# Soft-capped attention, feed-forward and routed experts on one Trainium2 core: expert tiles grouped into pairs, singles and small remainders, with a general path in a branch and constants made after the start

## The chip, the cores and the metric

The kernel runs on one core of one Trainium2 chip. The metric is the device time of one execution in microseconds. Lower is better. The time before is the median of three executions.

## The reference

Three stages follow each other. All data is float32.

```python
scores = cap * np.tanh(scale * (q @ k.T) / cap)          # 4 batches, 12 heads, 448 rows, 64 columns
attn = softmax(scores) @ v                               # -> x of 1792 tokens x 768
h = x @ w_in; x = (h * sigmoid(1.702 * h)) @ w_out       # 768 -> 2048 -> 768
logits = x @ w_gate; e_idx = argmax(logits, axis=1)      # 8 experts, each token goes to one
for e in range(8):
    mask = e_idx == e
    h = np.maximum(x[mask] @ w1[e], 0.0)                 # 768 -> 1024
    out[mask] = gate_w[mask, None] * eom[mask, e, None] * (h @ w2[e])   # 1024 -> 768
```

For the inputs that the reference makes, the eight experts get 616, 5, 21, 4, 710, 134, 3 and 299 of the 1792 tokens. Of the first 1344 tokens (three of the four batches) expert 0 gets 517. These counts are the reference's own `argmax`, counted.

## The kernel before

A planner (class `Plan`) puts every operation of the kernel into a static order for each engine. Each operation is added with a cost, a due time `v` shifted by a table `LEAD`, the operations it depends on and the ring buffers it uses. `run` fills the engines by due time. The order is fixed when the kernel is built, so on the chip each engine works through its list and waits for semaphores. Rings (`Ring(n)`) are buffers that are handed out in turn: user number c may start when user number c - n has finished.

The prologue (lines 384 to 445) runs before the planner's list. It makes constants: `zer`, `carry`, the identity, several scalars from the cap, `epst`, `fold`, `ones`, `tri` and eight ranges by `iota_f` (an iota on GpSimd, then a copy to float on VectorE, through one shared buffer). The first halves of q and k (`ld_qk`, line 565) come by one DMA of the SP queue and one of the ACT queue. The one on the ACT queue stands behind the activations of the prologue on that engine.

Attention and the feed-forward network are interleaved batch by batch. Float32 products are made as sums of three one-pass products: each operand is split into a rounded high part (`rnd_any`, line 477, ScalarE or VectorE) and a remainder (`rest_any`, line 485, VectorE), and high x high, low x high and high x low are added up in PSUM.

The routing of a batch (`route`) ends with running expert counts in `carry` and with scatters of token numbers into tables (line 1100). The experts' stage works in tiles of 128 tokens of one expert, called slots. `NSLOT` = 21 is the most that can be needed. Three full tiles (`NEARLY`) are picked after the third batch, and the others are enumerated after the fourth by a chain of small VectorE operations (`enumerate_tiles`, `expert_ids`, `token_ids`), sorted by expert. Slot number 21 is computed at the end under a branch (`tc.If`, line 1564, `last_slot`), which these inputs don't take. A second branch (line 1570) holds a whole second program for very large caps, not taken either.

One slot is:

- `slot_in`: an indirect gather of 128 token rows (line 1372), six transposes on TensorE (line 1392), a split of the result into two tiles `xT`.
- `l1`: for each of six chunks of the contraction, three products times two halves of 512 columns (line 1422, 36 matmuls), both halves side by side in two PSUM banks `psF`. Then ReLU (line 1435), eight transposes (line 1440), a split into two tiles `gT`.
- `l2`: for each of eight chunks three products times two halves of 384 columns (line 1472, 48 matmuls), in one PSUM tile `psO` of two banks. Then `out_y` (line 1479, ScalarE) and an indirect scatter (line 1482).

The expert's weights are loaded by conditional DMAs on the SP queue (`w_load`, line 1323): 3 of 1024 KB for `w1` and 4 of 768 KB for `w2`, into seven raw buffers that exist once each. The condition is a register that says whether the expert differs from that of the tile before. Each of the 14 chunks is split for every slot (`w_split`: 6 of 128x1024 and 8 of 128x768), into a ring of `WFB` + `MWB` = 4 + 5 buffers. The slots are staggered: `l1` of slot s is followed by `l2` of slot s - 1.

Of the kernel before, what the change touches and what calls it, by code (L numbers as in the profile page):

```python
# [9 lines left out]
F32 = mybir.dt.float32  # L10
F32R = mybir.dt.float32r
# [30 lines left out]
LEAD = {'tanh': 2.01, 'v_hi': 11.65, 'pv2': -12.5, 'tr': 5.5, 'x2_cp': -19.75, 'relu': -13.28, 'th': 16.62, 'g_hi': 18.86, 'x2_hi': 4.05, 'x2_lo': -8.67, 'transp': 14.31, 'w_s': -4.08, 'cap_max': -1.12, 'v_lo': 3.85, 'mms': 4.36, 'x2_tr': 4.06, 'pv_x': -6.73, 'scores': 6.33, 'q_hi': -30.03, 'lo': -8.55, 'ld_qk': 13.3, 'o_acc': -2.83, 'g_lo': -11.44, 'k_hi': 0.43, 'exp': 8.98, 'p_hi': 3.53, 'eps': -29.31, 'quantum': -3.73, 'w_e': 4.47, 'st_': 1.6, 'hi': 7.17, 'gmul': -12.05, 'pv1': -4.48, 'pv_add': 11.51, 'pv_cp': 22.53, 'p_lo': 13.02, 'logit': -9.76, 'norm': -11.99, 'x_hi': 5.57, 'out_y': -2.47, 'o_x2': -0.32, 'w_1': -3.42, 'w_2': -7.23, 'x_lo': 2.89, 'recip': -28.64, 'ld': -11.81, 'ld_v': 1.27, 'k_lo': 2.18, 'q_lo': 2.48, 'u_cp': -6.08, 's_ld': 6.02, 's_rc': -0.15, 's_st': -6.55, 'r_ld': -20.47, 'f': 17.0, 'v_f': 0.29}  # L42
TICK = 10.24 / 3
WFR = 2
W1 = 123.44
W2 = 218.024
W3 = 306.814
AF1 = 0.664
AF2 = 0.711
AF3 = 0.715  # L50
AO1 = -2.008
AO2 = -30.195
AO3 = 38.993
WLEAD = 22.922
RESTD = 1.01
POOLD = 0
# [5 lines left out]
ATT0 = 2.581  # L62
HID = 0.031
F3 = 157.954
NORMD = 0.877
NEARLY = 3
# [4 lines left out]
GATH = 10.0  # L71
WPRE = 14.0
# [3 lines left out]
VPL = 1.869  # L76
STG = -3.554
GL = 37.536
XIN = 11.584
HL = 10.021  # L80
XAL = 79.95
SPLIT = True
CV0 = 129.09
CV1 = 54.183
MWB = 5
SLOT = 17.899
# [28 lines left out]
class Plan:  # L115
# [10 lines left out]
    def __init__(self):  # L126
        self.tasks = []
        self.free = {"POOL": 5.0, "DVE": 4.5, "SP": 0.7}
        self.port = 0.0
        self.active = {}  # L130
# [209 lines left out]

@with_exitstack
def tile_softcap_attention_ffn_moe(
# [44 lines left out]
    nc.scalar.activation(carry, zer[:, :NE], AF.Copy)  # L387
# [20 lines left out]
    nc.scalar.activation(epst, ncapa, AF.Exp)  # L408
    nc.vector.tensor_scalar(out=epst, in0=epst, scalar1=1e-9, scalar2=None, op0=ALU.mult)
# [4 lines left out]
    nc.vector.tensor_tensor(out=fold, in0=ident[:32, :16], in1=ident[:32, 16:32], op=ALU.add)  # L414


    ones = const.tile([CK, 128], BF16, name="ones")
    nc.vector.memset(ones, 1.0)
    tri32 = const.tile([CK, CK], F32, name="tri32")
    nc.vector.memset(tri32, 1.0)  # L420
# [7 lines left out]
    def iota_f(name, p, pattern, base=0, cm=0):  # L428
        n = 1
        for _, k in pattern:  # L430
            n *= k
# [1185 lines left out]
```

## Time and profile before

| | us |
|---|---|
| median of 3 executions | 1145.5 |
| lowest and highest | 1144.22, 1148.94 |
| the profiled execution | 1141.25 |
| its span, first to last instruction | 1139.5 |
| mean granted TensorE clock (1 is 2.4 GHz) | 0.992 |

The profiled execution lasted 1.75 us longer than its span, and 4.25 us less than the median. Busy time of TensorE is not a measure of how much it could do, because matmuls overlap and their ends are modelled; the distance between their starts tells more.

### The profile page before, as it was taken

The numbers are of one execution on the slowest core, as the hardware profiler recorded it, in microseconds if no ns is written. First come the engines' busy times: TensorE is split into PE (matmuls) and PEld (weight loads), VectorE is DVE, ScalarE is ACT, GpSimd is POOL, SyncE is SP. The second block draws the span as 40 slices with busy tenths as digits, with TensorE's granted clock in tenths as the row PEclk, the third lists the DMA queues.
The fourth block names the chain that finished last, engine by engine and source line by source line (L and its number), as shares of the span: only waits on it lengthen the run. The fifth ranks groups of instructions, "written<-read, shape, count | busy, mean of one in ns | idle before, by whom it ended". The sixth has DMA issues, their size and how long they took to land. (4 is left out here: it accounts for less than half of the span.)

```text
span 1139.5 us, 16349 instructions
## 1 busy us (share of the span) xinstructions
PE 1090.1 (96%) x5378; PEld 918.4 (81%) x5378; DVE 933.4 (82%) x1606; ACT 779.3 (68%) x1308; POOL 209.7 (18%) x158
## 2 busy tenths in 40 slices
PE   5999999999999989999999999998999999999996
PEld 2455777778888878888888888977999898989986
DVE  4797999998897576697895645679999999999993
ACT  6998798787885353477882233347888787878873
POOL 0111001000000200100000102004623424243340
PEclk9999999999999989999999999999999999999999
DMA  6887678788887742744422535430279721347601
GB/s 177 213 233 199 196 201 253 223 238 242 267 245 247 146 117 81 160 119 113 127 87 86 118 127 210 179 112 24 69 262 377 276 101 43 120 152 289 253 1 37
DMA packets 70848, 191.37 MB, mean 168 GB/s; under 512 B 11950, under 2 KB 22494, under 8 KB 70752
## 3 DMA queue, kind: packets, MB, share of 16 engines
q1 hardware_dynamic: 63872, 170.79, 49.5%
q0 software_dynamic: 6656, 19.19, 5.2%
q8 instruction: 45, 0.74, 0.3%
q14 instruction: 51, 0.42, 0.1%
q10 hardware_dynamic: 224, 0.23, 0.1%
HBM read 238.86 MB, written 29.08 MB: 235 GB/s over the span
## 5 line engine op out<-in xcount | busy, mean ns | idle before, releaser
L971 PE MATMUL fps<-xh,w 128*128 128x448 f32 x384 | 146.8, 382 | 8.7 <-ACT w L477 8.2
L1482 POOL DMA_INDIRECT out_dram<-y,si x20 | 109.8, 5491 | 179.8 <-ACT y L1479 171.2
L971 PE MATMUL fps<-gh,w 128*128 128x448 f32 x384 | 142.2, 370 | 0.3 <-DVE th L995 0.3
L973 PE MATMUL fps<-xh,w 128*128 128x448 f32 x384 | 141.4, 368 | 0.3 <-DVE w L485 0.3
L972 PE MATMUL fps<-xl,w 128*128 128x448 f32 x384 | 141.4, 368 | 0.0
L972 PE MATMUL fps<-gl,w 128*128 128x448 f32 x384 | 140.8, 367 | 0.0
L973 PE MATMUL fps<-gh,w 128*128 128x448 f32 x384 | 140.2, 365 | 0.0
L485 DVE TENSOR_TENSOR w<-w 128x768 fp32r<-128x768 f32 (+1 forms) x98 | 104.1, 1068 | 42.7 <-ACT w L477 42.3
L646 ACT ACTIVATE p<-p,capx 112x448 f32<-112x448 f32 x192 | 126.9, 674 | 2.1
L642 ACT ACTIVATE p<-sps 112x448 f32<-112x448 f32 x184 | 97.2, 543 | 32.0 <-PE sps L638 17.4
L1472 PE MATMUL ops<-mw,gT 128*128 128x384 f32 x540 | 101.9, 339 | 0.0
L637 PE MATMUL sps<-qks 128*112 128x448 f32 x184 | 80.5, 437 | 21.5 <-ACT vf L477 12.1
L1422 PE MATMUL hps<-mw,xT 128*128 128x512 f32 x390 | 97.0, 399 | 0.0
L1472 PEld LDWEIGHTS ops<-mw,gT 128*128 128x128 f32 x540 | 93.2, 188 | 0.1
L477 ACT ACTIVATE w<-w 128x768 fp32r<-128x768 f32 (+1 forms) x78 | 71.8, 924 | 31.1 <-DMA w<-wsp 31.1
L971 PEld LDWEIGHTS fps<-xh,w 128*128 128x128 f32 x384 | 72.7, 189 | 22.1 <-ACT w L477 9.0
L477 ACT ACTIVATE mw<-w2r 128x768 fp32r<-128x768 f32 x79 | 67.0, 848 | 33.9 <-PE hps L1422 29.1
L1422 PEld LDWEIGHTS hps<-mw,xT 128*128 128x128 f32 x390 | 73.3, 191 | 14.9
L485 DVE TENSOR_TENSOR mw<-w2r,mw 128x768 fp32r<-128x768 f32 x90 | 82.1, 956 | 2.9 <-ACT mw L477 2.4
L1422 PE MATMUL hps<-w,xT 128*128 128x512 f32 x330 | 82.3, 398 | 0.0
L485 DVE TENSOR_TENSOR mw<-w1r,mw 128x1024 fp32r<-128x1024 f32 x65 | 77.1, 1220 | 5.6 <-ACT mw L477 5.6
L971 PEld LDWEIGHTS fps<-gh,w 128*128 128x128 f32 x384 | 72.1, 188 | 11.0 <-DVE th L995 0.6
(222 smaller groups left out, 2386.4 us busy)
## 6 DMA issues: line engine op xcount, KB each, us to landing
w1r<-in_w_dram SPq DMA_DIRECT2D x60, 1024.0 KB
w2r<-in_w_dram SPq DMA_DIRECT2D x80, 768.0 KB
w<-wsp SPq DMA_DIRECT2D x56, 384.0 KB
w<-wsp SPq DMA_DIRECT2D x42, 512.0 KB
qkr<-in_qk_dram SPq DMA_DIRECT2D x95, 224.0 KB
wr<-in_w_in_dram SPq DMA_DIRECT2D x32, 384.0 KB
wr<-in_w_out_dram SPq DMA_DIRECT2D x24, 512.0 KB
x2s<-x2tok SPq DMA_DIRECT2D x4, 1358.0 KB
```

The source lines that it names most:

```text
L477: nc.scalar.activation(o, i, AF.Copy)
L485: e.tensor_tensor(out=o, in0=x, in1=f32(hi), op=ALU.subtract)
L637: mm(sps, lhsT=t[:, 1, sl], rhs=t[:, 0, :], start=True, stop=False)
L642: nc.scalar.activation(p, T["s", kc], AF.Tanh, scale=sct2[:CK] if qkf else 1.0)
L646: nc.scalar.activation(p, p, AF.Exp, scale=capx[:CK])
L971: mm(fps, lhsT=wh, rhs=xh, start=c == 0, stop=False)
L972: mm(fps, lhsT=wh, rhs=xl, start=False, stop=False)
L973: mm(fps, lhsT=wl, rhs=xh, start=False, stop=c == n - 1)
L1422: mm(T["h", s][n], lhsT=x_[:, kk, :], rhs=w[:, a, n * 512:(n + 1) * 512], start=st_, stop=sp_)
L1472: mm(T["o", s][:, n, :384], lhsT=x_[:, k, :], rhs=w[:, a, n * 384:(n + 1) * 384], start=st_, stop=sp_)
L1482: nc.gpsimd.indirect_dma_start(out=out[:, :], out_offset=bass.IndirectOffsetOnAxis(ap=M[f"si{g}"][:, i:i + 1], axis=0), in_=T["y", s].rear ...
```

## The change

The experts' stage works in units that share one split of an expert's weights. A unit is a pair (P, two tiles of 128 tokens), a single (S, one tile) or a remainder (T, up to 64 tokens). Two pairs are picked after the third batch; after the fourth follow four groups of three units in the fixed order P T S, P T S, P T T, P T T. That is 14 tiles of 128 tokens and 6 remainders. The weights are loaded (if the expert changed) and split once for a unit.

A remainder is computed in two passes in place of three. Its high part fills stationary columns 0 to 63 and its low part columns 64 to 127 of one tile. One matmul gives high x high and low x high in separate rows, a second one of 64 columns adds high x low. The two sets of rows are added up by a matmul with `fold2` (first layer) or by VectorE (`low_y`, `sum_y`, `scaled_y`, second layer).

In every tile the second half of the columns runs two chunks behind the first (`AHEAD`), and each half has its own PSUM bank: `psO` has two single-bank buffers. The ring of split weights has 4 + 6 buffers. The enumeration after the fourth batch (`late_units`, `cumulate`, `find`) works on three lists of eight experts.

Tokens that the fixed units don't cover are found by `uncovered`; then a branch at the end computes all tiles again with 21 `last_slot` bodies. The branch for slot 21 is gone. With the counts above the units cover every token: expert 0 takes two early pairs and a single, expert 4 three pairs, expert 5 a single and a remainder, expert 7 a pair and a remainder, and the others a remainder each.

`epst`, `fold`, `ones`, `tri` and the ranges are made as tasks of the planner with due time 40 (`late_constants`); new constants (`fold2`, unit numbers as 52 one-column GpSimd memsets in groups of six) are made there too. The planner's tuned numbers (`LEAD`, stage lengths and offsets) are other values throughout, so the order of work in attention and feed-forward changes too.

```diff
-LEAD = {'tanh': 2.01, 'v_hi': 11.65, 'pv2': -12.5, 'tr': 5.5, ...
+LEAD = {'tanh': 3.35, 'v_hi': 13.94, 'pv2': -3.72, 'tr': 5.5, ...
...
-NEARLY = 3
+NPE = 2
+UNITS1 = [x for i in range(4) for x in ((i, "P"), (6 + i, "T"), ((4, "S"), (5, "S"), (10, "T"), (11, "T"))[i])]
+SLOTS1 = [(n, h, TS // 2 if k == "T" else TS) for n, k in UNITS1 for h in range(2 if k == "P" else 1)]
...
-MWB = 5
+MWB = 6
...
-    nc.scalar.activation(epst, ncapa, AF.Exp)
-    nc.vector.tensor_scalar(out=epst, in0=epst, scalar1=1e-9, scalar2=None, op0=ALU.mult)
...
+        constants = [] if general else late_constants(add, one)
...
-        psO = ms.enter_context(tc.tile_pool(name="psO", bufs=1, space=PSUM))
+        psO = ms.enter_context(tc.tile_pool(name="psO", bufs=2, space=PSUM))
...
+        order, lagging = [], []
+        for u in range(NPE):
+            order += [(1, s) for s in of_unit[u]] + [(2, s) for s in of_unit[u]]
+        for u in range(NPE, len(eunits), 3):
+            (a, b), (x,), (y,) = of_unit[u:u + 3]
+            order += [(1, a), (1, b)] + lagging + [(1, x), (2, a), (2, b), (2, x), (1, y)]
+            lagging = [(2, y)]
+        order += lagging
...
-        def w_split(kind, s, i):
+        def w_split(kind, u, i):
...
+        AHEAD = 2
+        def products(t, x, halves, width, k, nk, small):
+            for n, kk in ((0, k), (1, k - AHEAD)):
+                if not 0 <= kk < nk:
+                    continue
+                w = halves(kk)
+                o = slice(n * width, (n + 1) * width)
+                a, z = kk == 0, kk == nk - 1
+                if small:
+                    mm(t[n][:, :width], lhsT=x[0][:, kk, :], rhs=w[:, 0, o], start=a, stop=z, skip_group_check=True)
+                    mm(t[n][:TS // 2, :width], lhsT=x[0][:, kk, :TS // 2], rhs=w[:, 1, o], start=False, stop=z, skip_group_check=True)
+                    continue
+                mm(t[n][:, :width], lhsT=x[0][:, kk, :], rhs=w[:, 0, o], start=a, stop=False)
+                mm(t[n][:, :width], lhsT=x[1][:, kk, :], rhs=w[:, 0, o], start=False, stop=False)
+                mm(t[n][:, :width], lhsT=x[0][:, kk, :], rhs=w[:, 1, o], start=False, stop=z)
...
+                if small:
+                    x = add(one("ACT", c_act(384, 0.051)), low_y, v + 8, d, [ob[n], yb])
+                    x = add(one("DVE", c_dve(384)), sum_y, v + 8, [x], [ob[n], yb])
+                    ys.append(add(one("ACT", c_act(384, 0.19)), scaled_y, v + 8, [x, fin[s]], [yb, fcb[s]]))
...
-        with tc.If(nc.values_load(taken[0:1, 0:1], min_val=0, max_val=1) == 1):
-            last_slot(tc, nc, x2s, w1, w2, out, ident, M["gi1"][:, NSL - 1:NSL], M["si1"][:, NSL - 1:NSL], M["ei1"][0:1, NSL - 1:NSL])
...
+    left_out = nc.values_load(over[0:1, 0:1], min_val=0, max_val=1)
+    with tc.If(left_out == 1):
+        all_tiles(tc, nc, x2s, tab, w1, w2, out, ident, carry, eid, sid, rid, t128)
```

## Rows read from the trace of the kernel before

**Rows 1.** The page, part 1: busy us, share of the span, instructions, by engine

```profile
PE 1090.1 (96%) x5378; PEld 918.4 (81%) x5378; DVE 933.4 (82%) x1606; ACT 779.3 (68%) x1308; POOL 209.7 (18%) x158
```

**Rows 2.** Windows view: stretch, its length, busy us by engine, clock, DMA, GB/s; experts' slots

```profile
868.40:886.60 18.20, 18.20 (x99) 16.54 (x98) 17.18 (x21) 14.71 (x20) 6.97 (x3) 1.00 1.01 387
...
959.46:977.63 18.17, 18.17 (x100) 16.50 (x98) 17.16 (x21) 14.66 (x20) 7.00 (x2) 1.00 0.13 45
```

**Rows 3.** Chain of work that ended last: start, us, what; two runs of matmuls

```profile
808.28 4.20 PE ops L1472 x24
812.48 5.54 PE hps L1422 x24
```

**Rows 4.** Timeline of PE: start, us, operation; the eight transposes of a slot

```profile
880.15 1.04 PE L1440 MATMUL gtp<-ident,h 128*128 128x128 f32 x8
880.95 4.43 PE L1472 MATMUL ops<-mw,gT 128*128 128x384 f32 x24
```

**Rows 5.** Groups by line from 755 us: busy us, mean ns; weight splits

```profile
L485 DVE TENSOR_TENSOR mw<-w2r,mw 128x768 fp32r<-128x768 f32 x90 | 82.1, 956 | 2.9 <-ACT mw L477 2.4
L485 DVE TENSOR_TENSOR mw<-w1r,mw 128x1024 fp32r<-128x1024 f32 x65 | 77.1, 1220 | 5.6 <-ACT mw L477 5.6
L477 ACT ACTIVATE mw<-w2r 128x768 fp32r<-128x768 f32 x79 | 67.0, 848 | 33.9 <-PE hps L1422 29.1 <-PE ops L1472 3.6 <-ACT xT L477 0.6
L477 ACT ACTIVATE mw<-w1r 128x1024 fp32r<-128x1024 f32 x53 | 55.9, 1060 | 7.9 <-PE hps L1422 4.7 <-PE ops L1472 1.7 <-ACT xT L477 0.6
```

**Rows 6.** Timelines of ACT, SP queue, POOL and PE at the start

```profile
5.57 0.20 ACT L408 ACTIVATE epst<-ncapa 128x1 f32<-128x1 f32 x1 [3.25 <-DVE ncapa L402]
5.58 0.53 ACTq L565 DMA_DIRECT2D qkr<-in_qk_dram  x1
9.65 0.10 POOL L523 MEMSET vs<- 112x4 f32 x1
10.59 0.67 ACT L580 ACTIVATE qks<-qkr,sct 128x448 fp32r<-128x448 f32 x1 [4.82 <-DMA qkr<-in_qk_dram]
12.12 0.68 PE L637 MATMUL sps<-qks 128*112 128x448 f32 x1 [12.12 <-ACT vf L477]
```

**Rows 7.** Windows view, columns as in Rows 2: the first attention batch

```profile
30.00:60.00 30.00, 29.17 (x98) 14.31 (x97) 23.15 (x53) 29.61 (x61) 4.63 (x8) 1.00 0.85 220
```

**Rows 8.** Timelines of DVE and PE at the entry of the experts' stage

```profile
757.33 2.96 PE L1422 MATMUL hps<-w,xT 128*128 128x512 f32 x12
767.12 0.27 DVE L1542 TENSOR_TENSOR nt__7143<-carry,t 128x112 f32<-128x112 f32 x1
770.18 0.31 DVE L1228 TENSOR_TENSOR q<-o,jb 128x144 f32<-128x144 f32 x1
773.04 2.34 DVE L485 TENSOR_TENSOR mw<-w1r,mw 128x1024 fp32r<-128x1024 f32 x2
772.17 0.99 PE L1440 MATMUL gtp<-ident,h 128*128 128x128 f32 x4 [4.09 <-ACT h L1435]
```

**Rows 9.** Windows view, columns as in Rows 2: that entry

```profile
768.00:772.20 4.20, 0.11 (x2) 0.04 (x1) 3.72 (x18) 4.20 (x7) 3.15 (x4) 1.00 0.44 153
...
774.00:776.00 2.00, 2.00 (x7) 1.57 (x6) 2.00 (x3) 0.25 (x1) 0.00 (x0) 0.56 0.00 0
```

**Rows 10.** Timelines at the end: second layer behind second layer, last result

```profile
1122.38 2.35 PE L1472 MATMUL ops<-w,gT 128*128 128x384 f32 x12 [0.99 <-ACT y L1479]
...
1131.02 0.90 ACT L1479 ACTIVATE y<-ops,fc 128x768 f32<-128x768 f32 x1 [8.69 <-PE ops L1472]
```

**Rows 11.** One line's instructions: count, ns min/median/max, first and last start

```profile
L1564 POOLq COMPARE_BRANCH  x1: 65/65/65, 1132.5 to 1132.5; - x1
L1564 POOLq EVENT_SEMAPHORE  x1: 17/17/17, 1132.7 to 1132.7; - x1
L1571 POOLq EVENT_SEMAPHORE  x6: 17/30/43, 1136.3 to 1136.8; - x6
L1571 POOLq COMPARE_BRANCH  x1: 45/45/45, 1133.7 to 1133.7; - x1
```

More of the change, by code (lines that the diff above doesn't have):

```diff
@@ L71 @@
 GATH = 10.0
+CONSTV = 40.0
 WPRE = 14.0
@@ L443, in tile_softcap_attention_ffn_moe @@
     t128 = iota_f("t128", 128, [[TS, TPE]])
+    level = []
+    vid = iota_f("vid", 128, [[1, 3 * NE]])
+    eid3 = iota_f("eid3", 128, [[0, 3], [1, NE]])
+    uid0, uid, uidh, rows_ = (const.tile([128, n], F32, name=f"sl{i}") for i, n in enumerate((2 * NPE, NS1, NS1, NS1)))
+    for i in range(2 * NPE):
+        level.append((uid0, i, i // 2))
+    for i, (n, half, rows) in enumerate(SLOTS1):
+        level += [(uid, i, n), (uidh, i, n + half), (rows_, i, rows)]
+    t2 = iota_f("t2", 128, [[2, TPE // 2]], base=2)
@@ L1363, in slot_in @@
         def slot_in(s):
-            g, i = grp[s]
+            u, g, i, kind = slots[s]
+            small = kind == "T"
+            m = TS // 2 if small else TS
             v = at_l1(s)
@@ new lines, in product_tasks, with mms @@
+        def product_tasks(s, key, kind, nk, width, pool, tag, name, ring, xname, deps, uses, v):
+            u, _, _, sk = slots[s]
+            small = sk == "T"
+            fb = [ring.new(), ring.new()]
+            each = (2 if small else 3) * (0.231 if width == 512 else 0.174)
+            x, ends = None, []
+            for k in range(nk + AHEAD):
+                def mms(e, k=k):
+                    for n in range(2):
+                        if k == n * AHEAD:
+                            T.setdefault((key, s), []).append(pool.tile([128, 512], F32, tag=tag, name=name))
+                    products(T[key, s], T[xname, s], lambda kk: T["m", (kind, u, kk)], width, k, nk, small)
+                d = [x] if x else []
+                n, b = 0, []
+                if k < nk:
+                    d += deps(k) + wsplit[kind, u, k]
+                    n += 1
+                    b += [fb[0], wsb[kind, u, k]]
+                if k >= AHEAD:
+                    n += 1
+                    b += [fb[1], wsb[kind, u, k - AHEAD]]
+                x = add(one("PE", each * n), mms, v + 2 * each * k, d, list(dict.fromkeys(b + uses)))
+                if k in (nk - 1, nk + AHEAD - 1):
+                    ends.append(x)
+            return fb, ends
@@ L1426, in l1 @@
+            m = TS // 2 if small else TS
+            fb, ends = product_tasks(s, "h", 1, KD, 512, psF, "f", "hps", r_F, "xT", lambda k: list(xT_[s]) if k == 0 else [], [xTb[s]], v)
             hb = r_h.new()
-            gb = r_gT.new()
+            own = small and s in beside
+            gb = (r_gTx if own else r_gT).new()
             prev = []
@@ L1443, in hi @@
                     if n == 0:
[L1444 to L1448 removed]
+                        T["gT", s] = [pools["m2"].tile([128, 8, 128], F32R, tag="gTx" if own else f"gT{a}", name="gT", bufs=1 if own else 2) for a in range(1 if small else 2)]
```

552 lines of the change are left out of this document (372 added, 180 removed).

## The prediction

> **What bounds the kernel now.** I read the busy shares first: TensorE leads and VectorE follows [rows 1], but such a share says nothing of a single stage. The change lies in the experts' stage, so I cut that stage into windows of one slot. A slot takes 18.2 us, and it takes the same while the DMA engines are full (387 GB/s) and while they are nearly idle (45 GB/s) [rows 2]. TensorE is busy throughout, VectorE 17.2 and ScalarE 14.7 us. The starts of the matmuls say whether TensorE is really full: 24 of 512 columns take 5.54 us, 0.231 us each, and 24 of 384 columns 4.20 us, 0.175 us each [rows 3]. A slot has 36 of the first and 48 of the second kind: 8.31 + 8.38 = 16.69 us. Its 14 transposes at 0.10 us (eight between 880.15 and 880.95 us [rows 4]) are 1.4 us. The sum, 18.1, is the slot. So TensorE sets the pace in this stage, VectorE is 6% behind it, and loads are hidden even at 387 GB/s. The stage is 20 slots x 18.2 = 364.0 us.
>
> Outside the slots I looked for places where TensorE waits: the start [rows 6, 7], the entry of the experts' stage [rows 8, 9], and the end [rows 10, 11].
>
> **The change, part by part.**
>
> *Passes, -36 us.* The units hold 14 full tiles and 6 remainders in place of 20 full tiles. A full tile still has 84 matmuls and 14 transposes, so 18.2 us. A remainder has 24 + 32 matmuls of the same moving widths: 24 x 0.231 + 32 x 0.175 = 11.1 us. Its 14 small transposes and folds move 64 columns in place of 128; between half of 1.4 us and all of it I take 1.1, together 12.2 us. That makes 14 x 18.2 + 6 x 12.2 = 328.0 us, against 364.0. If a remainder's matmuls have costs that no row shows (two passes alternate 128 and 64 stationary columns), a unit might be 12.8 us, and the saving 32.4.
>
> *Splits, 0 where they are hidden.* They are made 14 times in place of 20. A unit's remainders cost VectorE 6 x 1.22 + 8 x 0.956 = 15.0 us, its high parts cost ScalarE 6 x 1.06 + 8 x 0.848 = 13.1 us [rows 5]. So 90 and 79 us fall away, all beside TensorE, which is why I count nothing for them. But the remaining splits are denser where remainders stand: a group P T T has 2 x 18.2 + 2 x 12.2 = 60.8 us of TensorE and 45 us of VectorE splits. VectorE's other work in a slot is 17.2 - 15.0 = 2.2 us [rows 2, 5], so for four tiles 8.8 us, in all 53.8. ScalarE has 39.4 and its other work, at most 14.7 x 4 minus four times 13.1, 6.4, in all 46; the additional result steps of a remainder raise this by a few us. Both fit on average. They are not free to run at all times: a pair's 8 chunks of `w2` stay in the ring of ten while its first tile is computed (8.4 us), and two buffers are left. I followed the ring through a P T T group by the durations above: the tightest place is a remainder's first layer followed by the next pair's, where 12 splits of 1.22 us (14.6 us) meet some 15 us of TensorE time. I take 2 us there (0 to 8).
>
> *Loads, 0.* The interleaved order changes the expert at nearly every unit: 13 loads of weights in place of 8, each 3 x 1 + 4 x 0.786 = 6.3 MB. At 387 GB/s [rows 2] one takes 16.3 us, three 49 us of the 61 to 67 us of a group. The cover is the window at 868 us, in which one load for each slot of 18.2 us costs nothing. If it is gone, see the rivals.
>
> *Bank hand-over, +4.5 us.* Now first layers follow first layers and second layers second layers, ten times in the latter case. The one such place before waits 0.99 us for `out_y` [rows 10]. There both halves share one tile; here the second half runs two chunks longer (6 x 0.175 = 1.05 us), which covers a result step of half the size if ScalarE is free, and it often has a split in hand. Between 0 and 0.99 I take 0.45 for each of ten places.
>
> *Entry, -2 us.* After the last count, VectorE works for 5.9 us (767.12 to 773.04) on the enumeration alone, and TensorE idles from 768.0 to 772.2 and then runs at a granted clock of 0.56, between half speed (1.2 GHz) and full [rows 8, 9]. The new chain: 31 steps on 8 to 112 elements at some 0.2, nine on 16 x 24 = 384 elements. Steps on 112 and 144 elements take 0.27 and 0.31 us [rows 8], a slope of 0.00125 us per element, so 0.6 us: 6.2 + 5.4 = 11.6 us, 6 us longer. Behind it on VectorE wait the splits, and TensorE waits for those. But the second tile of the first pair needs no new split, so 8.3 us of first layer fill what is now idle. Cover grows by 8.3, the chain by 6. I take -2, with 0 to -6 as ends. The chain is also queued in front of the first late gather and load, but these are wanted 72 us into the stage.
>
> *Start, -3 us.* The second q and k DMA is issued on the ACT queue at 5.58, behind `epst`, which waited 3.25 us; its data starts ScalarE at 10.59, the first matmul follows at 12.12 [rows 6]. Without `epst` in front the DMA can go after the table load and `carry`, at about 2.4. The landing takes 5.0 us, so ScalarE starts at 7.4 to 7.6. From then on ScalarE is full (29.6 of 30 us [rows 7]), so the 3 us are kept as long as that holds. The constants come back as tasks: some 20 VectorE instructions of 0.15 to 0.2 us and the GpSimd ones. VectorE has 6.9 us to spare in 30 us there, so they cost nothing. Ends: 0 and -4.
>
> One rule of the Trainium skill speaks against this last step. The trace shows a GpSimd memset of one column for four heads at 0.10 us [rows 6], and the change adds 52, 5.2 us at most. "SBUF — State Buffer", section "SBUF: two separate sides", says that VectorE in its two-port modes and GpSimd hold a shared port exclusively for a whole instruction. By that rule VectorE would lose up to 5.2 us; no row of before shows so many memsets beside attention. By the row the sum has 0 here, because ScalarE sets the pace.
>
> *End, +3.7 us.* The last two pieces are now first and second layer of one remainder with nothing between them: ReLU, fold, high and low part take some 2.5 us, of which the chunks that run behind cover one: +1.5. The last result takes three steps in place of one of 0.90 [rows 10]: +0.7. The hand-over of 0.99 us is counted above and goes here: -1.0. The branches: GpSimd passes the small one within 0.2 us (1132.5 to 1132.7), but the one over the whole second program takes 2.6 us (1133.7 to 1136.3) [rows 11], and the final barrier waits for that. The change has two large bodies to skip, so one of 2.6 in place of 0.2: +2.4. "Runtime: NRT & Kernel Launch", section "Instruction fetch mechanics", says the same of a taken branch that leaves the fetched pages; it adds nothing to the sum. Rounded: +3.7, ends 0 and 6.
>
> *Retuned order, 0.* All due times of attention and feed-forward move. No row can show a plan that hasn't run; from what TensorE idles before the experts' stage I give it 4 us either way.
>
> Sum: -36 + 2 + 4.5 - 2 - 3 + 3.7 = -30.8 us. Against the profiled execution this is 1141.25 - 30.8 = 1110.5; the median of before lies 4.25 higher, so I forecast 1145.5 - 30.8 = 1114.7, say 1115.
>
> **The rivals.**
> 1. *Splits don't run ahead.* If in each group the time in which the ring is full (some 4.3 us of the pair's first layer) is a wait for TensorE, four groups lose 17 us: 1132. For it: VectorE has 1 us to spare in 18.2 today. Against it: 90 us of its work go.
> 2. *Nothing new waits.* Hand-over, splits and end cost nothing, the entry gives its whole 6 us: 1145.5 - 36 - 3 - 6 = 1100.5.
> 3. *Slower: bare loads.* Each raw buffer exists once, so a unit's load waits for the splits of the unit before. If these are late, `w1` (3.1 MB, 8.1 us) is bare at each of 12 late units: 97 us, 1212. It is slower than before from 31 / 12 = 2.6 us of bare load for each unit. Against it: the window at 868 us, where the next expert comes in at the full rate of the DMA engines and the slot stays at 18.2 us [rows 2].
> 4. *The branch is taken.* If a count were other than I counted, 21 tiles follow in series, each at least 16.3 us of load: 342 us more, over 1450.
> 5. *The shared port.* 52 memsets hold VectorE, and ScalarE waits for it: +5.2 us, 1120. The rule named above is its ground; rows 7 speak against it.
>
> **How the numbers follow.** Forecast 0.75, rivals 0.10, 0.07, 0.04, 0.01 and 0.03 in order. The forecast's own ends reach from about 1104 to 1127; with the retuning and half of rival 1 the range for 8 in 10 is 1102 to 1130. Half a percent (1139.8 to 1151.2) is about what a measurement can tell from no change. Faster 0.93 (forecast, rivals 2 and 5, 0.08 of rival 1), same 0.02 (the rest of it), slower 0.05 (rivals 3 and 4).
>
> **What would show it.** Right: groups of 61 to 67 us with matmul starts 0.231 and 0.175 us apart; 196 splits in place of 280; the ACT-queue DMA near 2.4 and the first matmul near 9 us; an idle stretch at the entry no longer than today's; a second gap of some 2.6 us on GpSimd behind the last scatter. Wrong: TensorE waiting on VectorE's or ScalarE's `mw` inside the groups (rival 1), the SP queue's loads landing after the splits could start (rival 3), a first layer that starts later than 757 - 3 us (retuning), or `last_slot` lines in the trace (rival 4).

## The result, and the profile after

The changed kernel takes 1135.34 us (median of 4 executions, 1133.24 to 1137.44). The kernel before takes 1144.86 on the same chip (4 executions, 1142.76 to 1148.94). The ratio is 0.9917, 95% interval 0.989 to 0.9943. The kernel became faster, but by 9.5 us and not by the 30 that I forecast; 1135 lies above the range.

The two profiled executions are compared here: before 1141.25 us with a span of 1139.5, after 1137.44 with a span of 1135.7. They lie only 3.8 us apart, since the one of after is the slowest of its four, and the one of before is quicker than the four that were timed beside the changed kernel. So the table explains 3.8 us, and the medians differ by 9.5.

I cut both spans at the same places. "Entry" is the start of the first matmul into `hps`. "Pitch" is the usual distance from one start on TensorE to the next: 0.231 us behind a matmul of 512 columns, 0.175 us behind one of 384, 0.11 us behind a transpose, a fold or another small one. A "gap" is what a distance has beyond the pitch of its kind, counted where it is more than 0.03 us. With a limit of 0.1 us the stage without its gaps is 365.0 and 339.0, so its difference depends on the rule by about 1 us.

| us | before | after | difference |
|---|---|---|---|
| entry of the experts' stage | 757.3 | 766.1 | +8.8 |
| stage without its gaps | 359.8 | 332.7 | -27.1 |
| gaps in the stage | 13.7 | 26.0 | +12.3 |
| end of the last matmul to the end of the span | 8.7 | 10.9 | +2.2 |
| span | 1139.5 | 1135.7 | -3.8 |

The passes gave three quarters of what I expected. Two places took it back: the part ahead of the experts' stage, and gaps inside it. The first view is the page's list of busy times, the answer to [rows 1]. Every engine has less to do.

```profile
PE 1072.3 (94%) x5258; PEld 888.5 (78%) x5258; DVE 869.4 (77%) x1580; ACT 707.6 (62%) x1243; POOL 127.4 (11%) x214
```

The windows view, columns as in [rows 2], of 18 us near the begin of the stage and of 18 us in a group. TensorE is busy throughout, as in [rows 2]. VectorE is nearly full only while it makes splits.

```profile
793.00:811.00 18.00, 18.00 (x104) 17.14 (x103) 16.46 (x27) 9.28 (x14) 4.17 (x4) 1.00 0.52 178
868.00:886.00 18.00, 18.00 (x110) 17.23 (x109) 9.29 (x13) 9.35 (x16) 1.00 (x1) 1.00 0.58 196
```

Now the gaps. The timeline of TensorE at the three inner group ends (start, us, operation, and in brackets the idle time and what ended it):

```profile
907.50 0.44 PE L1660 MATMUL xtp<-ident,xg 128*128 128x128 f32 x2 [0.82 <-DVE xT L436]
976.12 0.50 PE L1693 MATMUL hps<-mw,xT 128*128 128x512 f32 x1 [1.16 <-ACT h L1740]
979.63 0.44 PE L1660 MATMUL xtp<-ident,xg 128*128 128x128 f32 x2 [1.42 <-DVE xT L436]
1048.66 1.70 PE L1747 MATMUL gtp<-fold,h 128*128 128x64 f32 x8 [3.65 <-ACT h L1740]
```

TensorE waits for ReLU (`h`) and for `xT`, not for a split. Both come from engines that work in order. The timeline of ScalarE at the same places says what stood ahead of them:

```profile
901.88 1.07 ACT L580 ACTIVATE w<-w1r 128x1024 fp32r<-128x1024 f32 x1 [3.20 <-DMA w1r<-in_w_dram]
973.14 1.06 ACT L580 ACTIVATE mw<-w1r 128x1024 fp32r<-128x1024 f32 x1 [3.95 <-DMA w1r<-in_w_dram]
1046.93 1.06 ACT L580 ACTIVATE mw<-w1r 128x1024 fp32r<-128x1024 f32 x1 [3.67 <-DMA w1r<-in_w_dram]
1048.01 0.60 ACT L1740 ACTIVATE h<-hps 128x512 f32<-128x512 f32 x1
```

At 1046.93 the high part of the next pair's first chunk has waited 3.67 us for its load. The ReLU that TensorE needs is queued behind it and runs at 1048.01. Why is the load late? The waits of the DMA queue of SP from 885 to 1060 us (what waits, for what: us in total, times, longest):

```profile
SPq L1589 <- DVE mw L588: 74.8, 26, 8.6
SPq L1589 <- DVE w L588: 48.9, 15, 11.1
```

The issue of a load waits for the split that frees its raw buffer. In the order `(2,x), (1,y)` the splits for `(1,y)` are the last ones that read the raw `w1` buffers, and the next pair's `(1,a)` follows at once. The load has no time left.

At the entry, the loss can be dated by counting the feed-forward matmuls of both traces. Up to the seventh group of 144 (400 us) the changed kernel is ahead by 3 to 12 us, at the twelfth (623 us) by 0.6. At the thirteenth (667 us) it is 8.2 behind. The view is the windows view of 645 to 665 us of after:

```profile
645.00:650.00 5.00, 5.00 (x26) 4.59 (x25) 2.56 (x5) 0.88 (x2) 0.00 (x0) 1.00 0.72 45
650.00:655.00 5.00, 2.10 (x11) 1.59 (x9) 0.72 (x2) 0.00 (x0) 0.00 (x0) 1.00 1.31 250
655.00:660.00 5.00, 0.00 (x0) 0.00 (x0) 0.00 (x0) 0.00 (x0) 0.00 (x0) 0.65 0.90 147
660.00:665.00 5.00, 3.89 (x10) 3.09 (x11) 2.24 (x3) 3.21 (x4) 0.00 (x0) 0.50 0.38 111
```

No engine works from 655 to 660, and then TensorE runs at half clock (0.50, so 1.2 GHz). The timelines of TensorE and of the SP queue of after show the wait and the order of the issues:

```profile
661.11 0.74 PE L1076 MATMUL fps<-xh,w 128*128 128x448 f32 x1 [9.01 <-ACT w L580]
...
637.84 0.37 SPq L1266 DMA_DIRECT2D x2s<-x2tok  x1
641.13 26.92 SPq L884 DMA_DIRECT2D w<-wsp  x5
```

GpSimd's timeline has the last of four indirect scatters of token numbers just ahead of that reload:

```profile
640.83 0.94 POOL L1205 DMA_INDIRECT tab<-tokid,posi  x1 [0.30 <-issue]
```

In the kernel before the same place costs 1.57 us:

```profile
650.61 0.47 PE L971 MATMUL fps<-xh,w 128*128 128x448 f32 x1 [1.57 <-ACT w L477]
```

The feed-forward weight that TensorE needs is read again from memory (`w<-wsp`) and issued behind the store of the tokens (`x2s`, 1358 KB) and behind the scatters to the table (`tab`). In the window 645 to 650 us the DMA engines count as 72% busy and move 45 GB/s.

At the start, the timelines of ScalarE's queue, ScalarE and TensorE answer [rows 6]:

```profile
1.30 0.55 ACTq L670 DMA_DIRECT2D qkr<-in_qk_dram  x1
...
5.42 0.67 ACT L685 ACTIVATE qks<-qkr,sct 128x448 fp32r<-128x448 f32 x1 [1.05 <-DMA qkr<-in_qk_dram]
...
6.95 0.68 PE L742 MATMUL sps<-qks 128*112 128x448 f32 x1 [6.95 <-DVE qks L700]
```

The first matmul comes 5.2 us earlier than in [rows 6]. The end follows, three of TensorE's last four waits (the first is a bank hand-over; the fourth, 0.70 us at 1113.96, is for a split):

```profile
1103.04 0.44 PE L1690 MATMUL ops<-mw,gT 128*128 128x384 f32 x1 [0.36 <-ACT y L1798]
...
1116.42 2.00 PE L1747 MATMUL gtp<-fold,h 128*128 128x64 f32 x16 [0.62 <-ACT h L1740]
1119.10 0.44 PE L1690 MATMUL ops<-mw,gT 128*128 128x384 f32 x1 [0.68 <-DVE gT L1761]
```

### The profile page after: what moved, and what is told of

It is laid out like the page before. It is cut to its first block, busy times and chain, and to the rows that moved or that the text cites. A ratio compares the mean times of both kernels' runs of the same rounds, so it can differ in the third digit from the quotient of the medians.

```text
span 1135.7 us, 15714 instructions
## 1 busy us (share of the span) xinstructions
PE 1072.3 (94%) x5258; PEld 888.5 (78%) x5258; DVE 869.4 (77%) x1580; ACT 707.6 (62%) x1243; POOL 127.4 (11%) x214
## 5 line engine op out<-in xcount | busy, mean ns | idle before, releaser
L742 PE MATMUL sps<-qks 128*112 128x448 f32 x184 | 79.8, 434 | 14.7 <-ACT p L747 7.7
L1076 PEld LDWEIGHTS fps<-xh,w 128*128 128x128 f32 x384 | 73.2, 191 | 21.6 <-ACT w L580 9.4
L1076 PEld LDWEIGHTS fps<-gh,w 128*128 128x128 f32 x384 | 72.5, 189 | 17.7 <-DVE th L1100 7.2
L1077 PEld LDWEIGHTS fps<-xl,w 128*128 128x128 f32 x384 | 73.3, 191 | 8.0 <-issue 1.9
L1078 PEld LDWEIGHTS fps<-gh,w 128*128 128x128 f32 x384 | 72.5, 189 | 7.6 <-DVE w L588 1.4
L1078 PEld LDWEIGHTS fps<-xh,w 128*128 128x128 f32 x384 | 73.0, 190 | 7.0 <-DVE w L588 0.5
L1077 PEld LDWEIGHTS fps<-gl,w 128*128 128x128 f32 x384 | 72.7, 189 | 6.3 <-issue 0.4
L588 DVE TENSOR_TENSOR mw<-w2r,mw 128x768 fp32r<-128x768 f32 x66 | 61.7, 954 | 17.5 <-ACT mw L580 16.5
L588 DVE TENSOR_TENSOR hl<-p,hl 112x448 fp32r<-112x448 f32 x112 | 69.2, 621 | 6.4 <-ACT hl L580 5.1
L1096 ACT ACTIVATE th<-fps 128x448 f32<-128x448 f32 x64 | 34.5, 539 | 60.7 <-PE fps L1078 60.5
L764 PE MATMUL pv<-p,vf 112*65 112x448 f32 x160 | 70.2, 543 | 0.8 <-ACT p L751 0.6
L743 PE MATMUL sps<-qks 128*112 128x448 f32 x184 | 69.2, 376 | 1.3 <-DVE qks L588 1.0
```

What stands on the lines that cost most here:

```text
L588: e.tensor_tensor(out=o, in0=x, in1=f32(hi), op=ALU.subtract)
L742: mm(sps, lhsT=t[:, 1, sl], rhs=t[:, 0, :], start=True, stop=False)
L743: mm(sps, lhsT=t[:, 2, sl], rhs=t[:, 0, :], start=False, stop=True)
L764: mm(T["pv", k], lhsT=VSh[:, c, :], rhs=T["p", kc], start=c == 0, stop=c == NC4 - 1)
L1076: mm(fps, lhsT=wh, rhs=xh, start=c == 0, stop=False)
L1077: mm(fps, lhsT=wh, rhs=xl, start=False, stop=False)
```

## The experiments

The questions: do the group ends cost what their gaps show, and is it the load? Is the late entry caused by the retuned numbers, by the earlier start or by the new work? Which of the smaller terms hold? All kernels ran beside the kernel before, in three groups, each on a chip of its own: e1, e2, e5 and e6; e9, e4, e3 and e11; e12, e13, e10 and e7. The kernel before had medians of 1145.78, 1144.13 and 1143.94 us there. So between groups, and against the changed kernel, a difference of medians also holds up to 1.8 us of the chips, and a step of 2 to 4 us lies inside overlapping intervals of the ratios. A table first; columns as in the table above, "no gaps" is the stage without its gaps, "tail" is what lies behind the last matmul.

| kernel | median us | ratio to before, 95% interval | entry | no gaps | gaps | tail |
|---|---|---|---|---|---|---|
| e1_no_late_loads | 1132.58 | 0.9885 (0.9849, 0.9922) | 762.6 | 332.6 | 21.3 | 11.1 |
| e2_front_numbers | 1128.72 | 0.9853 (0.9815, 0.9891) | 757.8 | 332.8 | 22.9 | 10.9 |
| e5_order | 1129.24 | 0.9857 (0.9813, 0.9901) | 765.5 | 332.1 | 18.1 | 11.0 |
| e6_order_front | 1120.44 | 0.9785 (0.9746, 0.9823) | 758.1 | 332.2 | 17.1 | 11.1 |
| e9_last_group | 1116.62 | 0.9765 (0.9731, 0.9799) | 756.4 | 332.2 | 14.5 | 11.2 |
| e4_early_constants | 1125.65 | 0.9848 (0.982, 0.9876) | 763.9 | 332.1 | 16.1 | 11.0 |
| e3_before_new_numbers | 1151.49 | 1.0069 (1.0043, 1.0094) | 769.3 | 359.9 | 12.3 | 8.6 |
| e11_store_on_act | 1123.75 | 0.9821 (0.9788, 0.9854) | 761.2 | 332.1 | 17.9 | 11.1 |
| e12_later_store | 1132.09 | 0.9899 (0.9852, 0.9946) | 759.7 | 332.6 | 23.6 | 11.1 |
| e13_order_front_store | 1114.26 | 0.9727 (0.969, 0.9765) | 754.4 | 332.3 | 14.6 | 11.0 |
| e10_no_cover | 1122.89 | 0.9816 (0.9778, 0.9854) | 757.8 | 332.5 | 18.3 | 11.7 |
| e7_no_fallback_body | 1119.02 | 0.9781 (0.9735, 0.9827) | 759.6 | 332.2 | 14.6 | 9.2 |

The column "no gaps" stays within 0.8 us in all that have the new units. What differs is the waits and the entry.

**Late loads taken away.**

```diff
-                lambda: nc.vector.tensor_copy(M[f"ei{g}"][:, n:], M[f"ch{g}"]),
+                lambda: nc.vector.tensor_copy(M[f"ei{g}"][:, n:], M[f"ch{g}"]) if g == 0 else nc.vector.memset(M["ei1"][:, n:], 0),
```

> The changed kernel (1135.3 us), with the change flags of the tiles picked after the fourth batch set to zero: the late conditional loads move nothing and the experts' tiles behind the first two pairs use expert 0's weights (left out: 12 of 13 loads of weights, 75 MB). Theory A (at the end of each group the next pair's w1 comes late, because its raw buffers are freed by the splits just before; ScalarE waits 3.2 to 4.0 us for the DMA and the ReLU stands behind it in order): the TensorE gaps of 2.3, 3.7 and 6.0 us at 907, 976 and 1049 us go, the experts' stage (766.1 to 1125.0 us, 358.9) falls to 346 to 350, time 1123 to 1127. Theory B (VectorE and ScalarE can't make the splits fast enough there, whatever the loads do): the gaps stay, time 1132 to 1136.

Of the four waits of TensorE shown above, 7.05 us in sum, one of 0.39 us is left, and ScalarE no longer waits for any `w1r` there. So the load is what made them. The time still falls into theory B's range, only 2.8 us under the changed kernel, because new waits appear at the entry, such as this one of TensorE:

```profile
795.00 0.20 PE L1531 MATMUL ptg<-ident,tg 16*128 16x16 f32 x1 [3.07 <-DVE tg L1527]
```

Why the entry waits more with fewer loads, I didn't settle. The stage also begins 3.5 us earlier than in the changed kernel, though the edit lies behind that point: its stall near 660 us is 6.32 us long in this execution. So much does one front vary.

**Before's numbers for attention and feed-forward.**

```diff
-W1 = 128.374
+W1 = 123.44
...
+        globals().update(FRONT)
         plan = Plan()
...
         r3 = ffn(len(halves) - 1)
+        globals().update(EXPERTS)
```

(`FRONT` holds before's `LEAD` and the stage numbers, `EXPERTS` the changed kernel's for the rest.)

> The changed kernel, with the numbers of the kernel before for attention and feed-forward (LEAD and the stage numbers); the experts keep the new ones. Theory C (the new numbers lose the 5 us won at the start and 9 more, in stalls at 400, 480 and 655 us): the experts' stage begins at 750 to 755 us in place of 766.1, time 1120 to 1126. Theory D (the lead is lost for another reason, such as the constants made later, and the numbers are innocent): it begins at 763 to 768, time 1132 to 1137.

The entry comes at 757.8, 8.4 us earlier than in the changed kernel, and the median falls by 6.6, less than theory C's range asks and more than D's. One execution of each is a narrow base for the 8.4. But the changed kernel, e1 and e5_order have the same front and enter at 766.1, 762.6 and 765.5, while the five kernels with this one (the last paragraph of this section lists them) enter at 757.9 on average: 6.8 us apart, with no overlap. The retuned numbers made the front later. But 757.8 is no better than before's 757.3, though the first matmul starts 5 us earlier: something else takes the early start back.

**Order at the group ends.**

```diff
-            order += [(1, a), (1, b)] + lagging + [(1, x), (2, a), (2, b), (2, x), (1, y)]
+            order += [(1, a), (1, b)] + lagging + [(1, x), (2, a), (2, b), (1, y), (2, x)]
```

> The changed kernel, with second layer of x and first layer of y exchanged in each group (..., (2, b), (1, y), (2, x)): splits of w1 and w2 then alternate all the way, and each raw buffer has the time of a whole unit's other layer to be loaded. Loads, splits and matmuls are as many. Theory A (late w1 loads at the end of a group): the three gaps shrink to under 1 us each, time 1123 to 1128. Theory B (split work too dense): the same work in the same time, 1132 to 1138.

With a second layer between `(1,y)` and the next pair TensorE has no wait left at the three group ends; the median falls by 6.1, to 1.2 us above theory A's range. A new wait comes at the end, where two second layers of remainders now stand back to back and share the banks of `psO`:

```profile
1106.39 0.44 PE L1690 MATMUL ops<-mw,gT 128*128 128x384 f32 x1 [3.09 <-DVE y L1805]
```

**Both.** The edit is the sum of the two above.

> Both edits of e2 and e5. If theories A and C hold and the places are apart, the gains add up: 10 + 13 us, time 1109 to 1116. If one of them falls, 1120 to 1128; if both, 1132 to 1138.

The gains add up: 1120.44, which is 14.9 us under the changed kernel, where the single ones give 6.6 and 6.1. That misses the range of 1109 to 1116, since each of the two was smaller than I had thought.

**The last group in the old order.**

```diff
-            order += [(1, a), (1, b)] + lagging + [(1, x), (2, a), (2, b), (1, y), (2, x)]
+            order += [(1, a), (1, b)] + lagging + [(1, x), (2, a), (2, b)] + ([(1, y), (2, x)] if u + 3 < len(eunits) else [(2, x), (1, y)])
```

> The kernel of e6_order_front with the last group alone back in the order of the changed kernel: ... (2,b), (2,x), (1,y). Nothing follows the last group, so no pair's splits wait behind its (1,y). Theory A (the order of (1,y) costs only where a pair's load needs the buffer that it frees): the gap of 3.45 us at 1098.99 and the half clock behind it fall back to what the changed kernel shows at its end (3.5 us of gaps in all), the three inner boundaries stay below 1.5 us each, and the time falls by 3 to 4 us, to 1116 to 1117.5. Rival (the end is bound by the chain from the last activation to the last store, whatever the order): within 1 us of e6_order_front, 1119.5 to 1121.5.

As theory A said: the wait at the end goes, the gaps fall by 2.6 us, the median by 3.8, to 1116.62. With these two repairs the change is near the 1115 of the prediction. That is in part luck: the passes gave 9 us less than forecast, the new waits in the front took the early start back, and the bank hand-over cost 4 us less.

**The constants back at the start.**

```diff
+    nc.scalar.activation(carry, zer[:, :NE], AF.Copy)
+    late_constants(lambda c, fn, v, deps=(), uses=(), **k: fn(next(iter(c))), lambda e, c, port=False: {e: c})
...
-        nc.scalar.activation(carry, zer[:, :NE], AF.Copy)
...
-        constants = [] if general else late_constants(add, one)
+        constants = []
```

> The kernel of e6_order_front with the constants (epst, carry, the masks and the memsets of the late list) made ahead of the first loads, as before's kernel does: the undo of the change's start. First matmul back near 12.1 us from 6.95. Theory C (the front's stalls on reloaded weights, at 400 and 650 us, swallow a lead that comes from the start): the 5.2 us are lost at the start and nothing at the entry of the experts' stage; entry 758 +/- 3 and time 1118 to 1122. Rival (the start's lead is kept to the end and the loss belongs to the retuned numbers alone): entry 761 to 763.5, time 1124 to 1126.

The rival is right. The first matmul moves to 13.12, the entry to 763.9, and the median is 5.2 us above e6_order_front. The early start is worth its whole 5 us. So the front of the changed kernel must contain new costs of about that size, and this run shows them without the lead. Its entry lies 6.6 us behind before's. The timelines of TensorE at the pick of the first units, of this run and of before:

```profile
713.28 0.23 PE L1537 MATMUL ptg<-ident,tg 4*128 4x4 f32 x1 [3.12 <-DVE tg L1533]
```

```profile
709.46 0.19 PE L1277 MATMUL ptg<-ident,tg 3*128 3x3 f32 x1 [1.61 <-DVE tg L1273]
```

And the windows view of both, first this run, then before:

```profile
640.00:680.00 40.00, 36.97 (x172) 33.00 (x171) 19.00 (x28) 13.59 (x19) 4.16 (x3) 0.96 0.59 137
...
714.00:717.00 3.00, 3.00 (x11) 2.67 (x10) 2.05 (x6) 0.54 (x1) 1.60 (x2) 0.57 1.01 407
```

```profile
640.00:680.00 40.00, 37.43 (x180) 33.13 (x179) 17.98 (x25) 12.12 (x18) 2.56 (x2) 1.00 0.54 130
...
710.00:713.00 3.00, 3.00 (x17) 2.76 (x16) 2.40 (x6) 0.00 (x0) 1.64 (x2) 1.00 1.02 411
```

The table lookup for the early pairs waits 1.5 us longer. Behind the wait of 3.12 us the granted clock is 0.57 for 3 us, behind before's 1.61 it stays at 1.00: 1.3 us more. By the counts of feed-forward matmuls this place loses 2.9 of the 6.6 us. Another 1.7 are lost from 640 to 680 us, with a clock of 0.96 and a wait for a reload that is 1.1 us longer (2.71 at 653.80). The other 2.0 are lost ahead of 640 us, 1.0 of them at the start.

**The new numbers alone, in the kernel before.**

```diff
-W1 = 123.44
+W1 = 128.374
...
```

> The kernel before with the retuned numbers of the change (lead times, windows and offsets of attention and the feed-forward part) and nothing else of it. Theory C (the new numbers themselves make the front later): entry of the experts' stage 5 to 9 us later than 757.3, time 1150 to 1154. Rival D (the new numbers cost only together with the earlier start and the new loads, for which they were found): entry within 3 us of 757.3, time 1142 to 1148.

The numbers make the kernel before slower by 7.4 us (interval 0.43% to 0.94%), and its entry 12 us later in the profile. The place is the same:

```profile
663.79 0.74 PE L975 MATMUL fps<-xh,w 128*128 128x448 f32 x1 [10.38 <-ACT w L481]
```

So the stall at 660 us belongs to the numbers, whatever comes behind it.

**The store on another queue.**

```diff
-            routed[b].append(add(c, lambda e: nc.sync.dma_start(x2s[b * S:(b + 1) * S, :].rearrange("(j p) w -> p j w", p=CK), T["tok", b]),
+            routed[b].append(add(one("ACT", 0.5), lambda e: nc.scalar.dma_start(x2s[b * S:(b + 1) * S, :].rearrange("(j p) w -> p j w", p=CK), T["tok", b]),
```

> The kernel of e6_order_front with the store of the tokens (x2s, 1358 KB) issued on ScalarE's queue instead of SyncE's, where the reloads of the feed-forward weights are issued behind it. Theory D (the reload's wait in SyncE's queue behind the store is what stalls the front near 400 and 650 us): the loads land within 6 us instead of 11 to 16, the stalls there shrink, entry 3 to 8 us earlier than 758.1, time 1113 to 1117. Rival (the transfer rate, not the place in the queue, is the limit there: the store's bytes move at the same time on the same engines): entry within 1.5 us of 758, time 1119 to 1122.

Neither: the stage begins 3.1 us later than in e6_order_front, and the median is 3.3 us higher. The stall near 400 us grows from 8.3 to 11.5 us, as the timelines of TensorE and ScalarE show; ScalarE waits 15.86 us for the reload:

```profile
403.80 0.74 PE L1080 MATMUL fps<-xh,w 128*128 128x448 f32 x1 [11.51 <-DVE th L1104]
...
401.38 0.84 ACT L584 ACTIVATE w<-w 128x768 fp32r<-128x768 f32 x1 [15.86 <-DMA w<-wsp]
```

Moving the store off SP's queue doesn't free the reloads, it delays them. That speaks against the place in SP's queue as the sole cause. "DMA: Bandwidth & Descriptors" of the Trainium skill, section "Queues, rings and completion order", says that each DMA engine takes packets in turn from the queues that have work for it, and in order within one ring. By that rule the reloads, now on a ring of their own, should take turns with the store and land earlier. The trace doesn't agree, and the measurement decides. From 382 to 391 us the DMA view of this run lists a single queue, ScalarE's (packets, MB, share of the engines):

```profile
q10 hardware_dynamic: 110, 0.34, 92.9%
```

The reload that went out on SP at 381.3 moves no packet in these 9 us, and the store itself moves 38 GB/s. Why, stays open.

**The store later.**

```diff
-            c, l = dma(1.4e6)
+            c, l = {"SP": (1.4e6 / DMAR, 20.0 if b < B - 1 else 0.0, False)}, DMAL
```

> The changed kernel with the stores of the tokens (x2s, 1358 KB, of all batches but the last) 20 us later in SyncE's order of issues: four to five more reloads of feed-forward weights (w<-wsp) go out ahead of each. The order of all else stays. Theory D, second form (the loads that TensorE needs at 400 and 660 us are late because they are issued behind the store, whose bytes and slow end they wait out; the retuned numbers issue fewer of them ahead of it): the gaps of 6.9 us at 407.56 and 9.2 us at 661.11 fall together by 6 to 12 us, the entry of the experts' stage comes at 755 to 760 in place of 766.12, time 1125 to 1130. Rival (the slow stretch comes with the four small scatters to the table, or with the number of reloads itself, wherever the store stands): the gaps stay within 3 us in sum, entry 763 to 769, time 1132 to 1138.

The store now goes out at 656.23. In the timelines of TensorE and of the SP queue the stall of 9.0 us is split into 2.3 and 2.3:

```profile
650.34 0.71 PE L1076 MATMUL fps<-xh,w 128*128 128x448 f32 x1 [2.33 <-DVE th L1100]
658.10 0.47 PE L1076 MATMUL fps<-gh,w 128*128 128x448 f32 x1 [2.27 <-DVE th L1100]
...
628.96 27.21 SPq L884 DMA_DIRECT2D w<-wsp  x7
656.23 0.42 SPq L1266 DMA_DIRECT2D x2s<-x2tok  x1
```

The gaps near 400 and 660 us fall from 16.1 to 10.3 us in sum, just short of the 6 us expected at least. The entry moves from 766.1 to 759.7, inside its range. In this one execution most of the late entry goes with the store's place ahead of the reloads.

But the rival holds in part: the slow stretch is there without the store. The windows view, 11 us before the store goes out, and GpSimd's last scatter ahead of it:

```profile
640.00:645.00 5.00, 5.00 (x27) 4.58 (x26) 1.80 (x4) 0.54 (x1) 0.00 (x0) 1.00 0.76 28
...
636.74 0.94 POOL L1205 DMA_INDIRECT tab<-tokid,posi  x1 [0.30 <-issue]
```

And near 400 us most of the stall stays, though the store now goes out behind the reloads that are late (first the changed kernel's wait, then this run's, and its store):

```profile
407.56 0.74 PE L1076 MATMUL fps<-gh,w 128*128 128x448 f32 x1 [6.79 <-DVE th L1100]
```

```profile
405.55 0.74 PE L1076 MATMUL fps<-gh,w 128*128 128x448 f32 x1 [5.24 <-DVE th L1100]
...
400.71 0.72 SPq L1266 DMA_DIRECT2D x2s<-x2tok  x1
```

So the store explains a part of the stalls. Near 650 us the slow stretch comes behind the four scatters in both kernels; no run leaves them out, so that they cause it isn't shown. The median falls by only 3.3 us, to the edge of the rival's range. Its four executions scatter from 1128.67 to 1137.44, and the intervals of both ratios overlap. In the time itself this gain isn't shown.

**The later store in the repaired kernel.** The same edit in e9_last_group.

> The kernel of e9_last_group (before's front numbers, (1,y) ahead of (2,x) but in the last group) with the same later stores. If theory D holds: the gaps of 8.15 us at 400.13 and 1.75 + 0.96 at 648 to 657 shrink by 5 to 9 us in sum, the 5 us of the earlier start reach the entry, entry 748 to 752, time 1108 to 1112. Rival: within 2 us of e9_last_group, 1114.5 to 1118.5.

1114.26 is the lowest time of all, 2.4 us under e9_last_group, but the two intervals overlap. The waits near 400 us go from 7.99 in e9_last_group

```profile
400.13 0.74 PE L1080 MATMUL fps<-xh,w 128*128 128x448 f32 x1 [7.99 <-ACT w L584]
```

to 1.21 and 3.00 in this one:

```profile
392.18 0.47 PE L1080 MATMUL fps<-xh,w 128*128 128x448 f32 x1 [1.21 <-DVE th L1104]
...
399.12 0.47 PE L1080 MATMUL fps<-xh,w 128*128 128x448 f32 x1 [3.00 <-DVE th L1104]
```

Near 650 us nothing is gained (2.7 us of waits against 3.0). The entry (754.4) gains 2 us of the expected 4 to 8, and the time misses its range.

**Without the two-chunk cover.**

```diff
-        AHEAD = 2
+        AHEAD = 0
...
-                if k in (nk - 1, nk + AHEAD - 1):
-                    ends.append(x)
+                if k == nk - 1:
+                    ends += [x, x]
```

> The kernel of e9_last_group with AHEAD = 0: the two halves of a tile's second layer are read out in the same step, so that the bank handed to the other half of the pair has no tile between. Theory of the prediction's hand-over term (without that cover each of some 10 hand-overs shows the whole eviction, 0.45 us more than with it or about 0.9 us in all): stage 4 to 9 us longer than 346.8, time 1120 to 1126. Rival (the hand-over is hidden by the other tile's first layer whatever the order, as the waits of 0.3 us in the changed kernel suggest): stage within 2 us of 346.8, time 1114.5 to 1118.5.

6.3 us slower, 4.0 of it in the stage, 0.5 in the tail, and 1.4 at the entry, ahead of what the edit touches. The time falls into the theory's range, but its mechanism doesn't show: TensorE's wait for a bank (`y`) is 0.2 us in the whole stage.

```profile
PE ops L1697 <- ACT y L1802: 0.2, 1, 0.2
```

The gaps are spread instead (`xT` 0.93 and 0.69, `gT` 1.51 in place of 0.68, splits 0.87 and 0.77). Why the order of the halves moves those, stays open.

**Without the fallback's body.**

```diff
     with tc.If(left_out == 1):
-        all_tiles(tc, nc, x2s, tab, w1, w2, out, ident, carry, eid, sid, rid, t128)
+        nc.sync.dma_start(out[0:1, 0:8], carry[0:1, :])
```

> The kernel of e9_last_group with the body of the last branch (the recomputation of all tiles, which is not taken) replaced by one small DMA. This run leaves that recomputation out. Theory (the longer end comes from the branch over that body, 2.4 us as the prediction had it): the stretch from the last matmul's end to the end of the span falls from 11.2 to 8.7 +/- 0.5 us, time 1113.5 to 1115. Rival (the end is the last stores' landing, the branch hides beside them): that stretch stays within 0.5 us of 11.2, time 1115.5 to 1117.5.

The tail is 9.2 in place of 11.2 us. The rows of the branch's line name the engine: first the changed kernel's branch on TensorE's load queue (count, ns min/median/max, first and last start), then this run's.

```profile
L1886 PEldq COMPARE_BRANCH  x1: 4312/4312/4312, 1130.2 to 1130.2; - x1
```

```profile
L1891 PEldq COMPARE_BRANCH  x1: 243/243/243, 1111.7 to 1111.7; - x1
```

4312 ns over the large body, 243 ns over one DMA. In the kernel before it is TensorE's queue too. GpSimd's branch over the second program takes 45 ns [rows 11], TensorE's this:

```profile
L1571 PEldq COMPARE_BRANCH  x1: 3355/3355/3355, 1131.6 to 1131.6; - x1
```

"Runtime: NRT & Kernel Launch" of the Trainium skill, section "Instruction fetch mechanics", says that a taken branch whose target isn't in the fetched pages forces a fetch; the two rows of this run and the changed kernel agree. The median didn't fall (1119.02 against 1116.62). In the profiled execution the entry is 3.2 us later, with a wait of 10.1 us near 400 us. Five kernels with the same front (e2, e6, e9, e10, e7) enter the stage at 757.8, 758.1, 756.4, 757.8 and 759.6, so 2 us in the tail can be hidden by that spread.

## Why the prediction was wrong

The sign was right, and the largest term came to three quarters. The 20 us that it missed (27 between the profiled executions) lie mostly in three steps: *Splits* with *Loads*, *Retuned order* and *Passes*. In the two profiled executions:

| step | predicted | measured | by |
|---|---|---|---|
| Passes | -36 | -27.1 | stage without its gaps |
| Splits and Loads | +2 | +10.6 | gaps from 800 to 1080 us: 17.1 in after, 6.5 at the same places in e6 and e9 (mean) |
| small gaps in the groups (no term) | 0 | +2.6 | the same stretch, 6.5 against 3.9 in before |
| Bank hand-over | +4.5 | +0.4 | TensorE's one wait for `y` |
| Entry | -2 | -3.4 | gaps at the entry: 8.0 before, 4.6 after |
| Start, and new waits ahead of the stage | -3 | +0.4 | entry of e2_front_numbers against before |
| Retuned order | 0 | +8.4 | entry of after against e2_front_numbers |
| End | +3.7 | +4.3 | tail +2.2, gaps at the end +2.1 without the wait for `y` |
| sum | -30.8 | -3.8 | spans |

*Passes.* The mechanism was right, the size of a remainder was off. Taking a full tile as 18.0 (before: 359.8 / 20), a remainder has (332.7 - 14 x 18.0) / 6 = 13.5 us, not 12.2. I had counted 14 small transposes and folds and priced them together at 1.1. There are 22, 6 transposes and 16 folds, and with half the columns they still start 0.11 us apart, so 2.4 us. The 16 folds alone are the row of 2.00 us at 1116.42. The six remainders miss 6 x 1.3 = 7.8 us, and another 1.2 go since a full tile takes 18.0 and not 18.2.

*Splits and Loads.* This step failed. The splits themselves became fewer as counted (the trace of after has the 196 remainders that I forecast). I followed the ring of split buffers through a group and looked for splits that come late. I put 2 us at the right place, a remainder's first layer followed by the next pair's. What came late there was the raw buffer. The load of a unit waits for the last split of the unit before, as I wrote in rival 3, and with `(1,y)` last in a group that split comes just ahead of the pair that needs the load. The cover that I named, the window at 868 us in [rows 2], was the wrong row: there one load has a slot of 18.2 us of other work ahead of it, and at the group end it has next to nothing. Rival 3 had this as 12 bare loads of 8.1 us; it happened at three places, with 3.2 to 4.0 us of waiting each. Rival 3's sign did appear there, a load that lands after its split could start. Rival 1's, TensorE waiting for `mw`, did not: the wait was ScalarE's, and TensorE waited for a ReLU queued behind it.

*Retuned order.* This step failed too. I wrote that no row could show it and gave it 4 us either way, from what TensorE idles ahead of the stage. It was 8.4 in these two executions. Both directions were tested: before's numbers in the changed kernel give 8.4 us at the entry (6.8 over all kernels with the two fronts) and 6.6 in the median, the new numbers in the kernel before cost 7.4 in the median. My sign for it, a first layer later than 754 us, appeared. The price was in sight: the stalls of 1.57 us at 650 us and of 6.67 us at 404 us in before show reloads that are just in time there. Counted in order, the reload that TensorE waits for near 650 us is in both kernels the first one behind the store. Its split starts 11.7 us after its issue in before and 19.1 us after it in the changed kernel. A later store gives a part of this back (e12_later_store); what makes the rest stays open.

*Start.* Right in kind, too small in size, and nearly nothing is left of it. ScalarE's DMA went out at 1.30 and the first matmul came at 6.95, for a gain of 5.2 us. e4_early_constants shows that its undo costs 5.2 us. But the front has new waits that I had no term for, 4.6 us of them at two places of that run (the early pairs' lookup, the reload, the clock behind both).

*Entry, End.* Right: -3.4 against -2, +4.3 against +3.7. The branch was the cause that I named, but on TensorE's queue: GpSimd's takes 45 ns in [rows 11], and I had taken the wait behind it for the branch.

*Bank hand-over.* Too dear: of 4.5 us 0.4 came. The change covers it, though the run without the two-chunk shift doesn't show that this shift is the reason.

*Rivals.* Rival 1's time (1132) was the nearest; its mechanism wasn't the one. The shared port (rival 5) has no sign, though no run tests it alone: the kernel with the late memsets is 5.2 us quicker than the one with all constants at the start. The branch wasn't taken.

## What to carry to other kernels

When work is regrouped, check at each new boundary the buffer that is handed over there, not the mean rate of its loads: which instruction frees it, how long before its next use, and what is queued in order behind the wait. The sign of a late load may be an engine further on, waiting for something that stands behind it. Retuned numbers of a planner are a part of a change like any other and can be put back alone; here the order with `(1,y)` ahead of `(2,x)` in all groups but the last, and the old numbers for the front, make 1116.62 us out of 1135.34.

## What the runs showed of the hardware that I had not expected

- DMA engines can count as busy and move little: 45 GB/s at 0.72 in 645 to 650 us of the changed kernel, behind four indirect scatters and a store of 1358 KB, and 28 GB/s at 0.76 in 640 to 645 us of e12_later_store, behind the scatters and ahead of the store. Reloads issued there land late. With the store on another queue they land later still (15.86 us of waiting).
- TensorE's branch over the fallback takes 4.3 us, and 0.24 us when the body is one DMA; on GpSimd the branch over a whole program takes 45 ns [rows 11].
- A wait of 3.12 us of TensorE (e4_early_constants) is followed by a granted clock of 0.57 in the next 3 us, a wait of 1.61 us at the same place (before) by 1.00.
